# Turning normalised tokens of three groups by 32x32 blocks on VectorE and through device memory, in place of TensorE turns

**Chip, cores, metric.** One core of one Trainium2 chip. The metric is the device time of one execution, in microseconds (us). "Clock" is the clock that TensorE was granted, 1.0 being full. Profiles are of single executions, so a span differs from the median of the runs: by 5.0 in before.

## The reference

Attention with decay, in chunks of 64 positions, for 4 batches of 768 tokens; its output is the input of a mixing block: a Fourier transform along the tokens and along the 512 features, added to the input, then a normalisation, then a perceptron of two layers.

```python
def _moe_ref(x, w_ch1, w_ch2):
    X = np.fft.fft(np.fft.fft(x, axis=1), axis=2)
    u = x + np.real(X).astype(np.float32)
    mu = np.mean(u, axis=-1, keepdims=True)
    var = np.mean((u - mu) ** 2, axis=-1, keepdims=True)
    un = (u - mu) / np.sqrt(var + 1e-06)
    ch = np.maximum(un @ w_ch1, 0.0) @ w_ch2          # 512 -> 2048 -> 512
    return (u + ch).astype(np.float32)
```

The kernels take `un @ w_ch1` with the features of the normalised tokens `un` on the partitions (L636 of the kernel before, pm<-ut,w), so each 128x512 tile is turned first. This change is about who turns it.

## The kernel before

Tokens come in groups of two 128-token tiles. The first four groups are "plain" (ordinary products); in order of use they are called first, second, third and fourth plain group. All later groups ("late") already take the way through device memory. The perceptron runs in two halves of its hidden width; the second weight's first half is converted from the given 64-bit form in 512-column pieces, whose last three are called c5, c6 and c7. The "folds" are VectorE's additions (L426 to L484) that prepare a batch's tokens for the Fourier transform, in a first and a second part.

```python
ep = front_pool("ep", 2)          # two tiles "e" in all
up = plain_pool("up", 3)          # turned tokens "ut", three tiles
...
def load_weights(dst, src):       # one piece; VectorE's and ScalarE's passes
    raw = hp_.tile(...); e = ep.tile([128, 2 * WP], U16, tag="e")
    pw, sg = ...                  # both lie in e
    nc.sync.dma_start(raw, src.bitcast(U32))
    nc.scalar.activation(sg, top.bitcast(I16), AF.Sign)                      # L216
    nc.vector.tensor_scalar(pw, top, 0x7FF0, ...)                            # L217
    nc.scalar.activation(pw, pw, AF.Relu, bias=cvt[:, 0:1], scale=8.0)       # L218
    nc.vector.tensor_tensor(p, p, sg, op=ALU.mult)                           # L220
    nc.vector.tensor_scalar(d, hi, 0x000FFFFF, 0x00100000, ...)              # L222
    nc.vector.scalar_tensor_tensor(dst, lo, 2.0 ** -32, d, ...)              # L224
    nc.vector.scalar_tensor_tensor(dst, dst, 2.0 ** -20, p, ...)             # L225
...
def norm(g):
    ...
    plain = (b, g) in PLAIN
    if plain: ut = uts[b, g] = new(up, [128, KO, G * 128], "ut")
    else:     to = utd[b, g] = dram.tile([128, KO, G * 128], F32)
    for i in range(G):
        un = ...                                                             # L564, VectorE
        if plain:
            pt = psum_a([128, KO, 128])
            for c in range(KO):
                nc.tensor.transpose(pt[:, c, :], un[:, 128*c:128*c+128], ident)   # L569
            nc.scalar.copy(ut[:, :, 128 * i:128 * i + 128], pt)              # L573
        else:
            uq = new(ep, [128, DM], "e")                                     # the same pool of two
            nc.vector.transpose(uq, un)                                      # L577
            for r in range(0, 128, 32):
                nc.sync.dma_start(dst, src)                                  # L581, four stores a tile
...
run(beside(mix, 24.0, beside(att1, 2.75 * t_chunk, w, 0.16 * NW), 0.16 * NW + 1.75 * t_chunk))
half = [[mlp(b, g, h * FO // 2, (h + 1) * FO // 2) for b, g in PLAIN[:3]] for h in range(2)]
```

A scheduler places the instructions on each engine when the kernel is built, and an edit in one place moves others (in x12, with eight stores off its queue, k is issued 27 us sooner than in x3). SyncE issues 225 of the 276 transfers of before, in one queue, one after the other.

## Time and profile before

| | before |
|---|---|
| median of 3 runs | 824.45 us (822.53 to 825.08) |
| profiled run, span | 819.4 us, clock 1.0 |
| TensorE busy | 795.2 us, 97% |
| turns on TensorE (L569) | 32, of which 24 are for the second to fourth plain group |

The prediction below shows the main rows. First, one stretch from the first turn of the first plain group to the first product of a late group, which does the same work in all kernels but for the turns, and leaves out the start, whose length varies (the first turn is at 91.91 us in x9 and at 95.46 in after). Columns: start:end, length, then busy time of PE, PEld, DVE, ACT and POOL with instruction counts, then clock, DMA share, GB/s.

```profile
92.88:428.13 335.25, 328.28 (x1907) 229.87 (x1907) 214.93 (x464) 87.20 (x207) 49.03 (x57) 1.00 0.42 111
```

TensorE idles for 335.25 - 328.28 = 6.97 us in it.

SyncE's queue before a later attention chunk:

```profile
181.24 0.38 SPq L263 DMA_DIRECT2D k<-in_k_dram  x1
```

TensorE takes this k at 192.32 us, 11.1 us after its issue.

### The profile page before, as it was taken

The page shows a single profiled execution, that of the slowest core. Times are in us where ns is not written, and L with a number is a line of the kernel's source. Part 1 is how long each engine was busy: PE and PEld are TensorE (multiplying, and loading weights), DVE is VectorE, ACT ScalarE, POOL GpSimd, SP SyncE. Part 2 cuts the span into 40 slices and gives each one's busy share as a digit, 9 for nine tenths or more (in the row PEclk, how much of TensorE's full clock was granted, in tenths as well). Part 3 has the DMA queues.
Part 4 walks back from the last instruction along what each step waited for, and adds up shares of the span by engine and source line. Part 5 has one row for each costly group of instructions (what it writes and reads, how often), then busy time and mean ns, then how long its engine had stood idle before and what let it go on. Part 6 is the DMA issues. An engine that isn't in the chain of part 4 may idle for free.

```text
span 819.4 us, 11694 instructions
## 1 busy us (share of the span) xinstructions
PE 795.2 (97%) x4608; PEld 634.9 (77%) x4608; DVE 437.8 (53%) x1018; ACT 186.5 (23%) x448; POOL 86.1 (11%) x102
## 2 busy tenths in 40 slices
PE   6989899999999999999999999999999999999998
PEld 5777767768585857768648888888888888888886
DVE  5899798766743761354895541165313661146311
ACT  3756344225420211312002200022001210022100
POOL 3223340011011010220000000000000000000000
PEclk9999999999999999999999999999999999999999
DMA  9979624248741136530351011100111001010010
GB/s 233 249 154 271 174 90 129 63 113 201 203 125 51 52 62 131 129 123 26 93 162 42 1 53 51 52 1 1 64 40 52 0 1 39 33 33 0 1 39 26
DMA packets 126684, 68.88 MB, mean 84 GB/s; under 512 B 111150, under 2 KB 112174, under 8 KB 126630
## 3 DMA queue, kind: packets, MB, share of 16 engines
q1 hardware_dynamic: 121488, 55.67, 26.6%
q0 software_dynamic: 2112, 6.69, 2.4%
q10 hardware_dynamic: 3030, 5.78, 1.9%
q8 instruction: 36, 0.59, 0.3%
q14 instruction: 18, 0.15, 0.1%
HBM read 48.72 MB, written 19.40 MB: 83 GB/s over the span
## 4 chain that ended last, share of the span: by engine, by line
PE 80%; DVE 10%; issue 4%; DMA 3%; ACT 2%; POOL 1%; POOLq 0%; ACTq 0%; DVEq 0%
PE p L770 24%; PE p L723 24%; PE pm L650 10%; PE pm L636 8%; PE pa L332 3%; PE pa L516 3%; PE pa L298 3%; DMA x<-xb,ix 2%; PE pa L328 2%; PE pa L274 1%; DVE sc L302 1%; PE pa L315 1%; PE pa L348 1%; PE pa L279 1%; DVE stt L546 1%
## 5 line engine op out<-in xcount | busy, mean ns | idle before, releaser
L636 PE MATMUL pm<-ut,w 128*128 128x256 f32 x512 | 119.2, 382 | 0.0
L650 PE MATMUL pm<-w,hr 128*128 128x512 f32 x256 | 115.8, 597 | 0.2 <-DVE w L225 0.2
L636 PEld LDWEIGHTS pm<-ut,w 128*128 128x128 f32 x512 | 94.4, 190 | 15.4 <-issue 3.6
L723 PE MATMUL p<-ur,w 128*128 128x256 f32 x384 | 93.8, 379 | 0.0
L650 PEld LDWEIGHTS pm<-w,hr 128*128 128x128 f32 x256 | 46.6, 190 | 49.5 <-issue 48.0
L723 PEld LDWEIGHTS p<-ur,w 128*128 128x128 f32 x384 | 73.0, 190 | 10.3 <-issue 0.5
L723 PE MATMUL p<-us,w1s 128*128 128x256 f32 x256 | 65.7, 379 | 0.0
L770 PE MATMUL p<-w,hs 128*128 128x256 f32 x256 | 58.0, 379 | 0.5 <-DVE y L791 0.5
L770 PE MATMUL p<-w2s,hs 128*128 128x256 f32 x256 | 57.9, 379 | 0.0
L770 PE MATMUL p<-w,ha 128*128 128x256 f32 x256 | 57.9, 379 | 0.0
L770 PEld LDWEIGHTS p<-w,hs 128*128 128x128 f32 x256 | 48.5, 190 | 7.5 <-DVE y L791 0.9
L625 POOL DMA_INDIRECT out_dram<-y,ix x12 | 11.9, 989 | 402.6 <-DVE y L796 342.6
L770 PEld LDWEIGHTS p<-w2s,hs 128*128 128x128 f32 x256 | 48.6, 190 | 6.6
L723 PEld LDWEIGHTS p<-us,w1s 128*128 128x128 f32 x256 | 48.6, 190 | 6.6
L770 PEld LDWEIGHTS p<-w,ha 128*128 128x128 f32 x256 | 48.6, 190 | 6.6
L750 ACT COPY ha<-p 128x256 f32<-128x256 f32 x32 | 11.9, 372 | 169.1 <-PE p L723 139.4
L761 DVE TENSOR_TENSOR ha<-p,ha 128x256 f32<-128x256 f32 x32 | 13.6, 424 | 45.2 <-ACT ha L760 45.2
L298 PEld LDWEIGHTS pa<-qT,kT 64*128 64x128 f32 x384 | 26.0, 193 | 13.2 <-ACT qT L281 7.3
L302 DVE TENSOR_TENSOR sc<-pa,decay 128x512 f32<-128x512 f32 x48 | 31.5, 683 | 8.8 <-PE pa L298 8.5
L332 PE MATMUL pa<-sc,v 128*64 128x128 f32 x384 | 32.1, 284 | 4.1 <-DVE sc L302 4.1
L298 PE MATMUL pa<-qT,kT 64*128 64x128 f32 x384 | 30.7, 292 | 3.2 <-ACT qT L281 2.9
L270 POOL TENSOR_TENSOR kd<-k,decay 128x512 f32<-128x512 f32 x20 | 23.0, 1152 | 94.8 <-PE pa L315 64.5
(144 smaller groups left out, 1135.0 us busy)
## 6 DMA issues: line engine op xcount, KB each, us to landing
raw<-in_moe_w_ch_dram SPq DMA_DIRECT2D x32, 512.0 KB, 4.8
k<-in_k_dram SPq DMA_DIRECT2D x24, 256.0 KB, 5.0
q<-in_q_dram SPq DMA_DIRECT2D x24, 256.0 KB, 5.9
v<-in_v_dram SPq DMA_DIRECT2D x24, 256.0 KB, 4.9
ud<-x SPq DMA_DIRECT2D x16, 256.0 KB, 2.3
utd<-e SPq DMA_DIRECT2D x64, 64.0 KB, 2.2
u<-ud SPq DMA_DIRECT2D x16, 256.0 KB, 2.7
ur<-utd SPq DMA_DIRECT2D x6, 512.0 KB, 4.3
```

Of the source, the lines that this page charges most:

```text
L270: nc.gpsimd.tensor_tensor(kd, kt, kpow, op=ALU.mult)
L298: mm(pss[hi][:, hp, :], lhsT=kT[HD[hi], hp, :], rhs=qT[HD[hi], hp, :], start=True, stop=True)
L302: nc.vector.tensor_tensor(t, pss[hi], decay[:, hi::2, :], op=ALU.mult)
L328: mm(po[HD[hi], hp, :], lhsT=s_old[HD[hi], hp, :], rhs=qs[HD[hi], hp, :], start=(hp == 0), stop=False, skip_group_check=True)
L332: mm(po[HD[hi], hp, :], lhsT=vt[:, 2 * hp + hi, :], rhs=sc[hi][:, hp, :], start=(c == 0 and hp == 0), stop=(hp == HP - 1), skip_group_chec ...
L516: mm = nc.tensor.matmul(ps[0:m, n, :], lhsT=piece(a, i, n), rhs=cs[0:rows, a, i in (2, 3), n, :], start=(a == 0), stop=(a == 1))
L625: nc.gpsimd.indirect_dma_start(out=out.rearrange("b s d -> (b s) d"), out_offset=row_of(2 + HC * (b + 1) + T - HC), in_=y[:, :], in_offset ...
L636: nc.tensor.matmul(ps, lhsT=w1[:, c, 128 * fc:128 * fc + 128], rhs=ut[:, c, :], start=(c == 0), stop=(c == KO - 1))
L650: nc.tensor.matmul(ps, lhsT=hr[(fc - f0) // 4][:, fc % 4, 128 * i:128 * i + 128], rhs=w2[:, fc, :], start=(fc == f0), stop=(fc == f1 - 1))
L723: nc.tensor.matmul(ps, lhsT=s2.A[a][:, kt, 128 * i:128 * i + 128], rhs=U[b][:, kt, :], start=(first and kt == 0), stop=(kt == 1), skip_gro ...
L761: V.tensor_tensor(a22, two(Z), a22, op=ADD)
L770: nc.tensor.matmul(ps, lhsT=h[a][:, s, i, :], rhs=s2.B[b][:, i, :], start=(first and i == 0), stop=(i == HF - 1), skip_group_check=True)
```

## The change

Intent: take 24 turns, and six copies out of accumulators, off TensorE and ScalarE. The second to fourth plain groups go the way of the late ones: VectorE turns 32x32 blocks (0.70 us for a 128x512 tile, L577), four stores a tile put the blocks in place in device memory (0.63 us each to issue, L581), and one fetch per group brings the turned tokens back when the perceptron nears them.

```diff
-            plain = (b, g) in PLAIN
-            if plain:
+            plain, turned = (b, g) in PLAIN, (b, g) == PLAIN[0]
+            if turned:
                 ut = uts[b, g] = new(up, [128, KO, G * 128], "ut")
@@
-                if plain:
+                if turned:
                     pt = psum_a([128, KO, 128])
@@
+    def fetch(n):
+        if n < len(PLAIN):
+            ut = uts[PLAIN[n]] = new(up, [128, KO, G * 128], "ut")
+            nc.sync.dma_start(ut, utd[PLAIN[n]])
+
     def mlp(b, g, f0=0, f1=FO):
         ut = uts[b, g]
+        n = PLAIN.index((b, g))
+        if f0 == 0 and n < 2:
+            fetch(n + 1)
+        elif f1 == FO and n == 1:
+            fetch(3)
```

(Not shown: the pin on the first turn, which keeps its meaning.)

More of the change, by code (lines that the diff above doesn't have):

```diff
@@ L569, in norm @@
                         mm = nc.tensor.transpose(pt[:, c, :], un[:, 128 * c:128 * c + 128], ident)
-                        if (b, g, i, c) == (*PLAIN[0], 0, 0):
+                        if i + c == 0:
                             tc.keep_in_program_order(mm)
```

## The prediction

> **What bounds the kernel now.** I read the page first (busy shares), then busy time by stretches of 20 us, then the chain that ended last between 100 and 170 us, then each engine instruction by instruction from 92 to 205 us, where three of the four plain groups (two 128-token tiles each) are turned.
>
> ```profile
> PE 795.2 (97%) x4608; PEld 634.9 (77%) x4608; DVE 437.8 (53%) x1018; ACT 186.5 (23%) x448; POOL 86.1 (11%) x102
> ```
>
> TensorE is busy for all but 24 of 819.4 us: what it is spared counts where it has no gaps, and every new gap counts in full. By stretches (start:end, length; busy PE, PEld, DVE, ACT, POOL; clock, DMA share, GB/s):
>
> ```profile
> 100.00:120.00 20.00, 18.31 (x89) 13.38 (x88) 17.34 (x44) 9.33 (x23) 8.56 (x6) 1.00 0.26 85
> 120.00:140.00 20.00, 19.82 (x77) 12.56 (x76) 18.66 (x46) 7.63 (x16) 1.10 (x1) 1.00 0.40 124
> 140.00:160.00 20.00, 19.06 (x102) 15.20 (x101) 13.83 (x33) 6.07 (x19) 1.89 (x4) 1.00 0.24 79
> 160.00:180.00 20.00, 20.00 (x119) 11.84 (x117) 15.98 (x36) 5.59 (x11) 2.72 (x4) 1.00 0.37 74
> ```
>
> From 100 to 140 us VectorE is nearly as full as TensorE (36.0 of 40 us), although it has 53% over the span: the change puts work on VectorE exactly where it has least room. The chain there confirms it:
>
> ```profile
> 127.47 0.60 DVE w L224
> 128.07 0.34 DVE fo L483
> 128.41 0.34 DVE fo L484
> 128.74 0.61 DVE w L225
> 129.36 0.04 issue
> 129.40 1.12 PE pm L650 x2
> ```
>
> TensorE's second-layer product at 129.40 waits for the last step of converting one 512-column piece of the second weight (call the last three pieces of its first half c5, c6, c7); VectorE runs without a gap up to it. The removed work on TensorE:
>
> ```profile
> 147.63 0.76 PE L569 MATMUL pa<-ident,un 128*128 128x128 f32 x4 [0.94 <-DVE un L564]
> 148.23 1.03 PE L636 MATMUL pm<-ut,w 128*128 128x256 f32 x4
> 149.10 0.60 PE L569 MATMUL pa<-ident,un 128*128 128x128 f32 x4
> 149.54 0.39 PE L529 MATMUL pa<-dt,ys 128*128 128x128 f32 x2
> ```
>
> Starts at 149.10 and 149.54 show that four turns occupy TensorE for 0.44 us, 0.11 each: the 273 ns of a group's mean is latency. The bracket is a gap of 0.94 us in which TensorE waited for the tokens. An ordinary product has two records.
>
> Last, what the new path costs where it exists already, for the late groups (first a row of operations with min/median/max ns, then two rows of issues, KB each, us to landing, then a wait on ScalarE):
>
> ```profile
> L577 DVE STREAM_TRANSPOSE e<-un x16: 682/700/712, 159.0 to 419.7; 128x512 f32<-128x512 f32 x16
> ```
> ```profile
> utd<-e SPq DMA_DIRECT2D x64, 64.0 KB, 2.2
> ur<-utd SPq DMA_DIRECT2D x6, 512.0 KB, 4.3
> ```
> ```profile
> 164.74 0.67 ACT L216 ACTIVATE e<-raw 128x512 bf16<-128x512 int16 x1 [2.12 <-DMA utd<-e]
> ```
>
> The last row is the one to keep: tiles named e come from a pool of two, shared by turned tokens and weight conversion. A conversion here stood still for 2.12 us until four stores had emptied an e.
>
> [...]
>
> **The change part by part.**
>
> Removed: 24 of 32 turns on TensorE, 24 x 0.11 = 2.64 us; six ScalarE copies of 0.59 us, on an engine that is 23% busy: nothing. Gaps before those turns: 1.04 (at 101.74), 0.64 (113.76) and 0.94 us (147.63), 2.6 together. Also freed: two accumulator banks which the fourth group's turned tokens hold from 149 to 246 us (their copies come at 245.83, when the first group's buffer is free). TensorE has no gap from 160 to 240 us, so this is worth nothing. The upper bound of the gain is about 5.2 us.
>
> Added: six VectorE turns (6 x 0.62 us in steady flow = 3.7 us), 24 stores on the SyncE queue (some 0.63 us each to issue), three fetches of 512 KB (4.3 us each). The fetches are issued early: the second group's would land at about 121, wanted after 124; the fourth's some 60 us ahead. Hidden.
>
> Moved: the built order shows that the scheduler brought the width products (L529 to L534) forward, ahead of the first group's first layer, and pushed the conversion of c5, c6, c7 back behind the turns of both groups. I worked that order through with the durations above. Steps on VectorE: 0.60 us for a 512-column pass, 0.335 for a half, 0.62 to 0.65 for a turn, 1.16 from the statistics over GpSimd to the scaling.
>
> TensorE: width products end at 98.0, 32 first-layer products of 0.43 us at 111.8, c0 to c4 for two tiles (10 x 0.86) at 120.4, so 4 us ahead of before.
>
> VectorE: statistics of the second group ready 100.3, its turns end 103.4 and 105.6; statistics of the third group 107.8, its turns end 111.4 and 112.7. The third group's first e is emptied by four stores issued from 111.5, landing at about 115.7 to 116.3, and only then does c5 start (0.4 for one pass, ScalarE's 0.7 + 0.72 beside it, then two VectorE passes): ready 118.2 to 118.9. c6 takes the same e after c5 and is woven with folds: ready 123.3 to 124.0. c7 comes behind both blocks of the second fold (some 20 passes, about 8.5 us) and two passes of the next piece: ready 135.2 to 135.9, before 129.3.
>
> So TensorE waits about 1.5 us for c6, and, having done one more product group, from 127 until 135.5 for c7: about 8.5 us. Against before it is then 6.2 us later with 0.86 us more done: 5.3 us behind. To 161 us it saves eight turns (0.9) and the gap of 0.94: about 3.5 us behind.
>
> Then 160 to 200 us. The fourth group's two turns and eight stores (8 x 0.63 = 5 us of SyncE) stand in the same in-order queue ahead of the other two groups' stores, two weight loads and the next k, q, v. In before those loads were issued at 181.2 and used at 192.3 after 5.0 us of landing: 6 us to spare. By the same working k is issued at about 189.5, lands at 194.5, wanted at about 193.5 to 194.5: up to 1 us. ScalarE's conversion passes wait for stores in front of the copies that free accumulators: 1 to 2 us more. I add 1.5 for this part.
>
> Sum: +3.5 + 1.5 = +5 us, 824.5 becomes about 829. After 240 us TensorE's order is the same product for product in both builds, so nothing further changes; the last two thirds only shift.
>
> **The rivals.** (a) The plain gain: the waits stay hidden, TensorE loses 2.6 us and some gaps: 819.5 to 822. For it: fetches have time, VectorE is at 53% over the span. Against: VectorE's 36 of 40 us just there, and the e pool of two. (b) Only the c7 stall, with later loads arriving in time: about 826 to 828. (c) The queue is worse than I worked out: [...]every k, q, v is late and attention runs with gaps: 833 to 840. Against it: each later load has several us of slack, and the queue catches up between chunks. (d) The freed banks let attention run ahead; worth nothing while TensorE is full.
>
> **Range and chances.** My sum rests on the c7 stall (6 us, whose length is mostly counted VectorE passes) less sure savings, so most weight lies on (b) and the sum, 825 to 832. (a) sets the low end at 820.5, (c) the high end at 837. Two per cent is 16.5 us: a gain of that size is not there (upper bound 5.2 us), chance 0.01; a loss needs all of (c), chance 0.04; within 2%: 0.95. Predicted 828.5.
>
> **What would show it.** Right: TensorE records of L569 drop from 32 to 8; TensorE busy sum falls by about 2.6 us while its gaps grow by about 7; gaps between 120 and 137 us before second-layer products, put down to the conversion passes; waits for utd stores of some 2 to 3 us at 112 to 116 us on VectorE and ScalarE; the second group's second layer starting 3 to 4 us later than 157.4. Wrong: if c7 is ready before 131 us, the stall step fails and (a) holds; if the first gap is before the second group's first layer, the fetch was not hidden; if the lag is made at 180 to 200 us instead, the queue was the matter; if it is made up again between 240 and 300 us, where 2.7 us of gaps exist, the shift was not rigid.

## More of the kernel before

Second, TensorE at the product with c7 (start, duration, engine, line, operation, tiles, shapes, count; in brackets the idle time before and what ended it):

```profile
129.40 1.12 PE L650 MATMUL pm<-w,hr 128*128 128x512 f32 x2 [0.17 <-DVE w L225]
130.36 2.79 PE L516 MATMUL pa<-cs,fe 128*128 128x193 f32 x16
```

Piece c7 is ready 0.17 us late: the schedule is tight, with nothing to spare.

## The result, and the profile after

| | before, same chip | after |
|---|---|---|
| median | 822.23 us (820.44 to 825.08, 6 runs) | 834.37 us (832.46 to 836.05, 6 runs) |
| profiled span, clock | 819.4 us, 1.0 | 833.9 us, 0.989 |

The ratio is 1.0139 (95% interval 1.0115 to 1.0164): slower by 12 us, but inside 2%. Ratios here are the mean time of one kernel's runs over the mean of the other's of the same rounds, so not quite the ratio of the medians.

The same stretch of after, from the first turn to the first late product:

```profile
95.46:442.35 346.89, 328.24 (x1884) 229.60 (x1883) 219.11 (x470) 84.93 (x201) 44.41 (x57) 0.98 0.45 116
```

It is 346.89 - 335.25 = 11.6 us longer, and so holds nearly the whole loss. TensorE's idle time in it grew from 6.97 to 18.65 us, by 11.7. Its busy time did not fall, although 24 turns are gone: the clock column says why, 0.98 in place of 1.00. Part of the work ran slower.

Where the idle time lies, TensorE after (rows with a gap, and the row behind the longest):

```profile
127.28 1.98 PE L660 MATMUL pm<-w,hr 128*128 128x512 f32 x4 [2.26 <-DVE w L225]
139.30 2.08 PE L660 MATMUL pm<-w,hr 128*128 128x512 f32 x2 [8.31 <-DVE w L225]
141.17 3.99 PE L516 MATMUL pa<-cs,fe 128*128 128x193 f32 x16
...
204.00 0.63 PE L274 MATMUL pa<-ident,k 128*128 128x128 f32 x4 [2.65 <-DMA k<-in_k_dram]
```

There are waits of 2.26 us for c6 and of 8.31 us for c7, both ended by the last pass of a conversion, and one of 2.65 us for the next chunk's k. With one of 0.76 us for ScalarE (not shown) they make 14.0 us. Compare the two rows behind the c7 wait with those of before: the same products took 2.08 in place of 1.12 us, and 3.99 in place of 2.79. The windows show the reason (second last columns: clock, DMA share, GB/s):

```profile
120.00:132.00 12.00, 8.73 (x24) 4.10 (x22) 11.09 (x27) 4.34 (x8) 0.00 (x0) 1.00 0.73 226
132.00:140.00 8.00, 0.70 (x1) 0.50 (x2) 8.00 (x21) 1.81 (x4) 0.00 (x0) 0.59 0.06 12
140.00:146.00 6.00, 6.00 (x21) 4.68 (x20) 5.93 (x14) 3.33 (x7) 0.00 (x0) 0.70 0.48 162
```

While TensorE stood idle the granted clock fell to half, and stayed there until 143.6 us. In windows of 1 us it is 0.5 or 1.0, with a mixture only where it changes. It is at half again from 205.1 to 208.5 us, behind the wait for k. Each window's busy time times (1 - clock), summed over the stretch, is 3.9 us lost while working; before has 0.0. After was at half clock in these three stretches before its end,

```profile
27.56:30.98 3.42, 3.42 (x23) 3.09 (x20) 2.88 (x7) 1.75 (x4) 0.67 (x1) 0.50 0.87 195
133.38:143.62 10.24, 4.32 (x10) 3.29 (x11) 10.24 (x27) 3.27 (x6) 0.00 (x0) 0.50 0.18 56
205.06:208.47 3.41, 3.41 (x15) 2.49 (x15) 3.08 (x7) 2.10 (x6) 0.01 (x1) 0.50 0.67 213
```

which are 3.42, 10.24 and 3.41 us long, one, three and one times 3.41 us, and start 105.82 and 71.68 us apart, 31 and 21 such steps. TensorE worked in them for 3.42, 4.32 and 3.41 us.

VectorE after, the rows that make the waits:

```profile
114.66 0.71 DVE L577 STREAM_TRANSPOSE e<-un 128x512 f32<-128x512 f32 x1
119.76 0.43 DVE L217 TENSOR_SCALAR e<-raw 128x512 uint16<-128x512 uint16 x1 [4.40 <-DMA utd<-e]
...
121.52 0.69 DVE L225 SCALAR_TENSOR_TENSOR w<-w,e 128x512 f32<-128x512 f32 x1
...
126.55 0.68 DVE L225 SCALAR_TENSOR_TENSOR w<-w,e 128x512 f32<-128x512 f32 x1
...
138.56 0.68 DVE L225 SCALAR_TENSOR_TENSOR w<-w,e 128x512 f32<-128x512 f32 x1
```

Read it from the top. The last turn of the third group fills an e. The conversion of c5 (L217) then idles 4.40 us until stores have emptied an e. The three L225 rows are c5, c6 and c7; between c6 and c7 VectorE has not one gap, but works off the second fold (30 rows left out here, 24 of them from L426 and the passes after it), which the scheduler now puts ahead of c7. So the e pool makes the first wait and VectorE's order makes the second.

SyncE after:

```profile
181.69 0.40 SPq L209 DMA_DIRECT2D raw<-in_moe_w_ch_dram  x1
190.64 5.70 SPq L581 DMA_DIRECT2D utd<-e  x8
...
197.58 0.39 SPq L263 DMA_DIRECT2D k<-in_k_dram  x1
```

Eight stores stand ahead of two weights and k. They are those of the batch's last late group; the fourth plain group's begin the sixteen at 159.82 us (not shown), since the tile `un` has one buffer and so the turns keep the program's order. From 182.1 to 190.6 us SyncE issued nothing: it waited for VectorE (first view, from the list of SyncE's waits: us, times, longest), until the first turn of that last group was done (second view):

```profile
SPq L581 <- DVE e L220: 8.8, 1, 8.8
```

```profile
189.91 0.71 DVE L577 STREAM_TRANSPOSE e<-un 128x512 f32<-128x512 f32 x1
```

(The profile names the pass beside the turn; the turn ends at 190.62.) In before this group's turns ran at 171.70 and 173.22. With a group more to turn, VectorE's built order has them behind the work of the next attention chunk. The eight issues then took 5.70 us: 0.63 each (median of all 88), and a wait for the second turn between them. So k was issued at 197.58 and TensorE got it at 204.00.

### The profile page after: what moved, and what is told of

Same layout as the page of the kernel before. It is cut to its first block, busy times and chain, and to the rows that moved or that the text cites.

```text
span 833.9 us, 11694 instructions
## 1 busy us (share of the span) xinstructions
PE 796.9 (96%) x4584; PEld 636.1 (76%) x4584; DVE 443.3 (53%) x1024; ACT 183.9 (22%) x442; POOL 81.7 (10%) x102
## 5 line engine op out<-in xcount | busy, mean ns | idle before, releaser
L646 PEld LDWEIGHTS pm<-ut,w 128*128 128x128 f32 x512 | 94.9, 190 | 16.7 <-issue 3.3
L302 DVE TENSOR_TENSOR sc<-pa,decay 128x512 f32<-128x512 f32 x48 | 31.3, 685 | 11.7 <-PE pa L298 11.6
L332 PE MATMUL pa<-sc,v 128*64 128x128 f32 x384 | 32.9, 290 | 4.4 <-DVE sc L302 4.3
L298 PEld LDWEIGHTS pa<-qT,kT 64*128 64x128 f32 x384 | 25.1, 193 | 14.0 <-ACT qT L281 6.9
L332 PEld LDWEIGHTS pa<-sc,v 128*64 128x64 f32 x384 | 24.2, 142 | 12.2 <-DVE sc L302 6.1
L298 PE MATMUL pa<-qT,kT 64*128 64x128 f32 x384 | 29.8, 291 | 3.7 <-ACT qT L281 2.9
```

The costliest lines, as they stand in the source:

```text
L298: mm(pss[hi][:, hp, :], lhsT=kT[HD[hi], hp, :], rhs=qT[HD[hi], hp, :], start=True, stop=True)
L302: nc.vector.tensor_tensor(t, pss[hi], decay[:, hi::2, :], op=ALU.mult)
L332: mm(po[HD[hi], hp, :], lhsT=vt[:, 2 * hp + hi, :], rhs=sc[hi][:, hp, :], start=(c == 0 and hp == 0), stop=(hp == HP - 1), skip_group_chec ...
L646: nc.tensor.matmul(ps, lhsT=w1[:, c, 128 * fc:128 * fc + 128], rhs=ut[:, c, :], start=(c == 0), stop=(c == KO - 1))
```

## The experiments

Twelve kernels ran, and all give the reference's result. Theory A, stated first: the loss is made by added work in two orders that had little slack (none before c7, some 6 us before k). VectorE's order and the pool of two e delay c5 to c7; SyncE's order delays k. Its rivals are named where they are tested. Medians of before, on the chips concerned: 821.3 us for x1 to x4 (7 runs), 820.8 for x5 to x8 (7 runs), 822.7 for x9 to x12 (11 runs).

### x1: turned tokens in tiles of their own

The second and third group's turned tokens go to free tiles of the ut pool; only the fourth's stay in e.

```diff
+            own = (b, g) in PLAIN[1:3]
+            if own:
+                uqs = new(up, [128, KO, G * 128], "ut").rearrange("p c (i n) -> p (c i n)", i=G)
@@
-                    uq = new(ep, [128, DM], "e")
+                    uq = uqs[:, DM * i:DM * i + DM] if own else new(ep, [128, DM], "e")
```

> The changed kernel, but the turned tokens of the second and third plain group go into free buffers of the ut pool, not into the pool of two tiles e which the weight conversion uses too; the fourth group's still go into e. Theory A (the conversions of c5 to c7 stand behind the turned tokens' stores because they share e): VectorE's wait of 4.4 us before c5 is gone, TensorE's gap before c6 (2.26 us) too, the gap before c7 (8.31 us) falls to 3 to 5 us because c7 still stands behind the folds; median about 827. Theory B (the six turns' time on VectorE is enough by itself): the gaps before c6 and c7 stay within 1.5 us of 10.6 together, median 833 to 835.

Measured: 829.26 us (826.08 to 832.37, 4 runs), ratio 1.0083 (1.0057 to 1.0109). TensorE:

```profile
119.44 7.11 PE L663 MATMUL pm<-w,hr 128*128 128x512 f32 x16 [1.88 <-DVE w L225]
131.41 2.07 PE L663 MATMUL pm<-w,hr 128*128 128x512 f32 x2 [3.13 <-DVE w L225]
```

Without the shared tile VectorE's 4.40 us wait is gone and the c7 wait fell from 8.31 to 3.13 us, in the expected range; theory B falls. The c6 wait (first row) did not go, as was expected, but is 1.88 us: c6 came 5.6 us sooner, counted from the first turn, but the scheduler also put its first product after six products in place of twelve. The time came out 2 us above the expectation, and its runs spread over 6 us. They follow the clock roughly: 826.08 us at a mean clock of 0.996, 828.34 at 0.996, 830.18 at 0.994, 832.37 at 0.989. In the profiled run, the slowest, the half clock lasted from 130.5 to 140.7 us, so that sixteen products took 5.35 us and not 2.79. The shorter wait thus cost more in lost clock: behind its 3.13 us TensorE worked at half clock from 131.4 to 140.7 us, about 4.7 us lost by these times, against 2.2 us lost behind the 8.31 us of after.

### x2 and x3: only some of the groups

x2 moves the second and third group and leaves the fourth on TensorE; x3 does the opposite.

```diff
-   plain, turned = (b, g) in PLAIN, (b, g) == PLAIN[0]
+   plain, turned = (b, g) in PLAIN, (b, g) in (PLAIN[0], PLAIN[3])    # x2; in x3: in PLAIN[:3]
```

(and the fetches of the groups concerned)

> Only the second and third plain group are moved; the fourth is turned by TensorE as before. Theory A with its second part (the fourth group's stores hold the next k behind them in the SyncE queue): the gaps before c6 and c7 stay at 10 to 11 us, the gap of 2.65 us before the k transposes near 200 us is gone, and so are the slow products after it; median 829 to 831. If the k gap comes from the lag of the first part, it stays, and the median is 833 to 835.

> Only the fourth plain group is moved; the first three are turned by TensorE as before. Theory A: no gap before c6 and at most 1 us before c7, as before; k late near 190 to 200 us by 1 to 3 us; median 822 to 826. If the fourth group's move is harmless by itself, 820 to 822.

Measured: x2 833.83 us (830.49 to 837.21, 4 runs), ratio 1.0143 (1.0102 to 1.0184); x3 825.34 us (824.99 to 827.14, 4 runs), ratio 1.0055 (1.0038 to 1.0073). TensorE in x2, then in x3:

```profile
125.86 2.81 PE L658 MATMUL pm<-w,hr 128*128 128x512 f32 x4 [2.15 <-DVE w L225]
137.89 2.08 PE L658 MATMUL pm<-w,hr 128*128 128x512 f32 x2 [6.62 <-DVE w L225]
```

```profile
193.38 0.63 PE L274 MATMUL pa<-ident,k 128*128 128x128 f32 x4 [2.34 <-DMA k<-in_k_dram]
```

The two losses part cleanly: the waits for the conversion come with the second and third group, the wait for k with the fourth. In x2 the gaps were as expected and the time was 3 to 5 us above: half clock cost 8.1 us while working, as in x1 (8.1): 6.4 us in the stretches from 126.9 to 130.3 and 133.7 to 147.4 us, and 1.7 more from 307.8 us, after a gap of 1.58 us far from the change. No expectation so far had priced the half clock behind the c7 wait; x5 tests it.

### x4: the added work without the gain

The kernel before, still turning on TensorE, with VectorE's turns and the stores of the three groups added for nothing, and no fetch. Rival C holds that the fetches come late and hold TensorE up; here there are none.

```diff
                     nc.scalar.copy(ut[:, :, 128 * i:128 * i + 128], pt)
+                    if (b, g) != PLAIN[0]:
+                        uq = new(ep, [128, DM], "e")
+                        nc.vector.transpose(uq, un)
+                        for r in range(0, 128, 32): ... nc.sync.dma_start(dst, src)
```

> The kernel before, with the turn on VectorE and its stores added for the three groups for nothing: TensorE still turns them and nothing is fetched. Theory A says that what is added costs and what is removed saves little: gaps before c6 and c7 as in the changed kernel, median 834 to 839. Theory C (the fetched tokens come late, so TensorE waits for the round trip through device memory): no fetch, so the median stays at 822 to 826.

Measured: 837.96 us (836.18 to 839.74, 4 runs), ratio 1.0209 (1.0186 to 1.0231). The two long waits are there, 8.71 us before c7 and 2.79 us for k, put down to the same releasers as in after. The one before c6 is not: TensorE, which still has its turns to do, comes later.

So C falls. x4 is 16.7 us above its own before, after 12.1 above its own: 4.5 us apart, about what the saved turns can be worth (4.2, below). In the profiles x4 lost less to half clock, 1.6 us against 3.9.

### x5: work in the gap

Nine products for nothing, pinned between the c6 and the c7 products of the changed kernel. Theory H: the idle stretch is what halves the clock. Rival J: the clock dips for another reason.

```diff
             for fc in range(f0, f1):
+                if (b, g, i, fc) == (*PLAIN[0], 0, 7):
+                    pf = psum_a([128, DM])
+                    for k in range(9):
+                        mm = nc.tensor.matmul(pf, lhsT=hr[0][:, 0, 0:128], rhs=w2[:, 0, :], start=True, stop=True)
+                        tc.keep_in_program_order(mm)
```

> The changed kernel with nine products of 128x512 for nothing on TensorE (about 0.87 us each, 7.9 us together), pinned between the c6 products and the c7 product, where TensorE idled for 8.3 us; nothing else changed. Theory H (the idle stretch before c7 is what halves TensorE's granted clock for the next 4 us): the gap before c7 shrinks from 8.3 us to under 2, the granted clock stays 1.0 from 130 to 150 us, the sixteen fold products there take 2.8 us and not 4.0; the time falls by about 2 us, to 832 (830 to 835), although the work has grown. Rival J (the clock dips for other reasons[...] and would dip as much with the gap filled): the half-clock stretch near 140 us is still there, and the fillers run in it; the time is that of the changed kernel, 834, or more.

Measured: 832.03 us (831.38 to 833.48, 4 runs), ratio 1.0125 (1.0092 to 1.0159).

```profile
126.37 1.12 PE L665 MATMUL pm<-w,hr 128*128 128x512 f32 x2 [2.08 <-DVE w L225]
127.34 7.89 PE L663 MATMUL pa<-w,hr 128*128 128x512 f32 x18
...
138.39 1.12 PE L665 MATMUL pm<-w,hr 128*128 128x512 f32 x2 [0.58 <-DVE w L225]
139.35 2.79 PE L516 MATMUL pa<-cs,fe 128*128 128x193 f32 x16
```

```profile
132.00:140.00 8.00, 7.42 (x24) 4.18 (x23) 8.00 (x21) 1.84 (x5) 0.00 (x0) 1.00 0.36 108
140.00:146.00 6.00, 6.00 (x35) 5.10 (x34) 5.53 (x14) 3.69 (x8) 0.00 (x0) 1.00 0.36 118
```

With 7.9 us of useless work added, the c7 product is back at 1.12 us and the sixteen fold products at 2.79. H holds, J falls. In time, the interval overlaps that of after, so the gain of some 2 us is not settled by the runs. The clock is, and not in one profile alone: the mean clock is 0.996 to 0.998 in all four runs, and 0.989 to 0.994 in all six of after. This profile had a dip of its own, 70 to 74 us, before the change's place, after a gap of 1.29 us.

### x6 and x8: one more piece converted early

To get c7 ahead of the second fold, one more piece is converted in an earlier stage, in the changed kernel (x6) and, as a control, in the kernel before (x8). The turned tokens of x6 are still in e.

```diff
-    run(beside(mix, 24.0, beside(att1, 2.75 * t_chunk, w, 0.16 * NW), 0.16 * NW + 1.75 * t_chunk))
+    run(beside(mix, 24.0, beside(att1, 2.75 * t_chunk, w, 0.2 * NW), 0.2 * NW + 1.75 * t_chunk))
```

> The changed kernel with one more weight piece converted in the stretch before the folds (share 0.20 of the weights in place of 0.16), so that in VectorE's order c7 stands before the second fold and not behind it; the turned tokens still share e. Theory A (VectorE's order and the two tiles of e make the stall): the c7 gap falls from 8.3 to under 3 us, since c7's conversion no longer waits behind the second fold, though c5 or c6 still wait for the stores by up to 4 us in e; 826 to 831. Rival (the stall is the device-memory path itself, and moves with it): the gap stays at 6 to 9 us and the time at 833 to 836.

> The kernel before with the same earlier conversion and nothing else: the control for x6 and x7. Its small waits before c5 to c7 are already under 1 us, so both theories expect no more than 1 us of change, 820 to 823. If it falls by 2 us or more, what x7 gains over the kernel before is the conversion's place and not the moved turns.

Measured: x6 833.25 us (827.88 to 833.44, 4 runs), ratio 1.0118 (1.0071 to 1.0164); x8 826.50 us (825.75 to 827.76, 4 runs), ratio 1.0054 (1.0022 to 1.0085). Both times missed. In x6 the c7 wait is gone (0.53 us is left), so VectorE's order was indeed what made it. But k, which waited 2.65 us in after, now waits 6.51:

```profile
200.87 1.09 PE L274 MATMUL pa<-ident,k 128*128 128x128 f32 x4 [6.51 <-DMA k<-in_k_dram]
```

Counted from the first turn, TensorE came to k's place 6.3 us sooner than in after and k only 2.5 us sooner: most of a wait removed in one place stood up again in the next. And the early piece has a price of its own, which x8 shows alone. Its control expectation, "no more than 1 us", was wrong: TensorE waits for the first normalised tokens,

```profile
94.25 0.67 PE L569 MATMUL pa<-ident,un 128*128 128x128 f32 x4 [2.94 <-DVE un L564]
...
97.39 1.97 PE L328 MATMUL pa<-qs,st 64*64 64x128 f32 x14
```

and then works at half clock from 95 to 102 us (3.3 us lost). VectorE's order at this place is the same in before, conversion passes included. What differs is TensorE's: in before it fills this time with the attention's products,

```profile
90.00 1.09 PE L328 MATMUL pa<-qs,st 64*64 64x128 f32 x16 [0.75 <-DVE qs L285]
```

which in x8 the scheduler put behind the turns.

### x7: the same, without the shared tiles and without the fourth group

x1's own tiles, x2's choice of groups, x6's early piece.

> Only the second and third plain groups moved, their turned tokens in free buffers of their own pool, and one more weight piece converted before the folds: every cost that theory A names is taken away (no wait for stores in e, c7 before the second fold, no late k). The 16 turns (1.8 us) and some of their gaps leave TensorE. Theory A: no gap of over 1.5 us on TensorE from 105 to 210 us, granted clock 1.0, 818 to 821, the first version below the kernel before (821 to 822). If the gain of the removed turns is worth nothing on this path: 821 to 824.

Measured: 825.62 us (824.51 to 825.71, 4 runs), ratio 1.0046 (1.0015 to 1.0077). From 105 to 210 us its largest gap is 1.00 us, as expected; the miss of 5 us is x8's price, a gap of 2.57 us and half clock from 92 to 99. Against its control x8 it is 0.9 us shorter, which the runs do not tell from none.

### x9 and x10: the extra piece in a better place

The extra piece comes after the first plain group's tokens: x9 is otherwise x7, x10 is the kernel before. Rival K: VectorE's added turning comes back as a wait whatever the order.

```diff
+    run(part(w, 1.0))
     half = [[mlp(b, g, h * FO // 2, (h + 1) * FO // 2) for b, g in PLAIN[:3]] for h in range(2)]
```

> As x7 (only the second and third plain groups moved, their turned tokens in free buffers of their own pool), but with the extra weight piece converted after the first plain group's normalised tokens and not ahead of them, where in x7 and x8 it made TensorE wait 2.6 to 2.9 us at 92 to 94 us and then run some 6 us at half clock (3 us lost). In VectorE's order c7 still stands before the second fold. Theory A: no gap over 1.5 us from 85 to 210 us, no half clock there, and the 16 turns' 1.8 us with some of their gaps gained: 818 to 821 against 821 before. Rival K (VectorE's added 2.8 us of turning reappear as a wait of 1.5 to 3 us at c5 to c7, whatever the order): 821 to 825.

> The kernel before with the same later place of the extra piece: the control of x9. Its c5 to c7 waits were under 1 us, so nothing is to be gained: 820 to 823. Its wait for the first normalised tokens should be at most 1 us (2.9 in x8).

Measured: x9 820.49 us (818.78 to 822.89, 6 runs), ratio 0.9980 (0.9957 to 1.0002); x10 821.59 us (820.57 to 822.87, 6 runs), ratio 0.9987 (0.9965 to 1.0009). The largest gap of x9 between 85 and 210 us is 1.12 us, before a product with a piece of the second weight, and there is no half clock. K falls. The second and third group then gain about 1 us over the control, which the runs do not tell from none.

### x12 and x11: k's queue

x12 is x3 with the fourth group's eight stores issued by GpSimd. x11 is the changed kernel with all three groups moved and everything mended: own tiles, the extra piece as in x9, and these eight stores on GpSimd.

```diff
-                        nc.sync.dma_start(dst, src)
+                        (nc.gpsimd if (b, g) == PLAIN[3] else nc.sync).dma_start(dst, src)
```

> As x3 (only the fourth plain group moved; 825.3 us, with a wait of 2.34 us for k and 3.8 us at half clock after it), with that group's stores issued by GpSimd in place of SyncE. If k is late because eight issues of 0.71 us stand ahead of it on SyncE's queue: no wait for k over 1 us, no half clock, 820 to 822. If its landing is late: unchanged, 824 to 827.

> All three groups moved as in the changed kernel, with every named cost mended: own buffers for the second and third group, the extra piece as in x9, and the fourth group's eight stores issued by GpSimd, so that the next k stands behind none of them on SyncE's queue. Theory A with the k step: the waits at c5 to c7 and for k are each under 1 us, no half clock from 85 to 210 us, 24 turns (2.6 us) and their gaps (up to 2.6 us) gained: 816 to 820. Rival: k stays late (the landing, not the issue, is what is late[...]): a gap of 2 to 3 us with half clock after it, 821 to 826.

Measured: x12 818.59 us (817.86 to 821.74, 6 runs), ratio 0.9953 (0.9929 to 0.9977); x11 818.67 us (818.24 to 819.43, 5 runs), ratio 0.9950 (0.9927 to 0.9974). Both are below the kernel before, by half a per cent, and x12 below its expected range. Three of the 11 runs of before are at a mean clock of 0.996 and took over 825 us; the other eight have a median of 822.4 us, and the control x10 has 821.6, so the gain without half clock is 3 to 4 us. SyncE in x3, then in x12 (x3's eight stores are again the last late group's; the sixteen of x12 are those of both late groups):

```profile
180.34 5.70 SPq L581 DMA_DIRECT2D utd<-e  x8
...
187.29 0.38 SPq L263 DMA_DIRECT2D k<-in_k_dram  x1
```

```profile
160.47 0.38 SPq L263 DMA_DIRECT2D k<-in_k_dram  x1
...
165.64 15.21 SPq L581 DMA_DIRECT2D utd<-e  x16
```

The wait for k is gone. But the step is not the clean one expected: k is issued 27 us sooner, not 5.7, since with eight stores off its queue the scheduler also put k ahead of the late groups' sixteen stores. TensorE takes this k sooner too, at 185.13 us (192.32 in before). That k stood behind those stores is shown as the cause of its wait; that the fourth group's eight issues are any part of it is not. Issue time alone was not the matter in after: SyncE waited 8.8 us for the data of the stores ahead of k, and the eight issues took 5.70 us. The stores took no less time to land (3.2 us from GpSimd, 2.2 from SyncE).

The same stretch as above, first turn to first late product, in the profiles of x9, x10, x11 and x12:

```profile
91.91:425.87 333.96, 326.32 (x1892) 228.47 (x1892) 216.15 (x469) 83.83 (x202) 44.28 (x57) 1.00 0.45 116
```

```profile
92.07:427.53 335.46, 328.36 (x1907) 229.84 (x1907) 214.32 (x465) 86.66 (x206) 49.75 (x57) 1.00 0.42 109
```

```profile
93.30:425.52 332.22, 324.55 (x1883) 226.56 (x1883) 217.07 (x471) 82.74 (x200) 50.84 (x65) 1.00 0.47 120
```

```profile
94.05:425.93 331.88, 325.59 (x1899) 228.39 (x1899) 216.33 (x466) 85.56 (x205) 55.09 (x65) 1.00 0.44 115
```

Against before's 335.25 us: -1.3, +0.2, -3.0, -3.4. In x11, TensorE's busy time fell by 3.7 us for 24 turns, and idle time grew by 0.7. x12 gains as much with only 8 turns moved; summed by operation its busy time shows 1.4 us less of turns, and about 1.3 us less in the attention's products (L298 and L332), as x11's does. Why those are shorter is open. x11's 16 further turns take 2.5 us more off TensorE, but it idles 1.4 us longer than x12 and its other products count 1.5 us more; why is open. No run gives the kernel before an earlier k alone, so how much of the gain of x11 and x12 is the moved turns' is not shown.

## Why the prediction was right and wrong

The time, 834.4, lies in the stated range of 820.5 to 837 and within 2%, as forecast. That is in part luck: it is above 825 to 832, where most of the weight lay, and in the band of rival (c), every k, q and v late, which did not happen. The mechanism was right in the main: waits for the conversion, put down to VectorE, and no trouble with the fetches. The loss was too small: +5 predicted (from 824.5, 2 us above the 822.2 of the later runs), +12 measured (+11.6 in the stretch, which is used here). Each step, counted from the first turn so that the start's noise drops out:

- **TensorE ahead at c0 by 4 us.** Right. The first second-layer product came 23.3 us after the first turn in before and 19.1 in after.
- **The e pool, c5 and c6: 1.5 us of wait.** Right in kind, 2.26 in size. VectorE stood still for 4.40 us, where the working allowed about 3, so c5 and c6 came near 1 us later than worked out.
- **c7 behind the second fold: 8.5 us of wait, 5.3 us behind.** The wait was 8.31. Counting VectorE's passes in the built order gave it. TensorE was 43.84 - 36.52 = 7.3 us later, with 0.9 more done: 6.5 behind.
- **From there to 161 us only savings, 3.5 us behind.** This step failed. The gap of 0.94 and eight turns were saved as said, but the c7 wait halved TensorE's clock until 143.6 us, 2.2 us lost, and at the third marker (the second group's second layer) after was 70.90 - 64.48 = 6.4 us behind. The prediction priced a gap at its length; x5 shows that a gap also slowed what followed (the c7 product took 2.08 us behind the gap and 1.12 with the gap filled).
- **k up to 1 us late, 1 to 2 us on ScalarE's copies: 1.5.** This term was mis-sized most. The wait for k was 2.65 us. The stores' issue time was right, 0.63 us. But the last late group's stores began 15.6 us later than in before, behind a turn that VectorE's order had put late, so k was issued 13.8 us later (102.12 against 88.36) where the working had 8.3; TensorE was ready for it only 6.5 us later (105.89 against 99.44); and k needed 6.4 us from issue to use where 5.0 was allowed. Nothing in the prediction has SyncE waiting for that turn. ScalarE's share was 0.76. With 1.7 us of half clock behind it the place cost 5.1 us, 3.6 more than the term. This is what rival (c) had named, the queue, although not with k, q and v late in every chunk: one chunk was.
- **Removed: 24 x 0.11 = 2.64 us.** Too low by the trace's count. TensorE's busy time for turns fell by 4.2 us (5.7 for 32 in before, 1.5 for 8 in after), about 0.17 each. This counts each group of four to its end, which may overlap what follows (in the prediction's rows 0.60 us from 149.10, with the next start at 149.54). All of TensorE's busy time in the stretch, less the half clock's 3.9 us, fell by about as much, 3.9.
- **A rigid shift after 240 us.** Right: after is behind by 14.1 us at 269 us, 14.2 at 428 and 14.5 at the end, of which 2.6 are the start's.
- **Rival (d), the freed accumulator banks, worth nothing.** No run contradicts it, none isolates it.
- **The stores' 2.2 us to landing.** Right for the stores that SyncE issues: 2.2 us in after as well (median). The eight that GpSimd issued in x12 took 3.2 us.

The sum that closes: idle time +11.7, half clock +3.9, turns -4.2, together +11.4 against 11.6 measured. (Idle and busy time make up the stretch by definition; what this tests is the split of the busy time.) By place, what the predicted +5 lacked: 1.2 up to c7, 1.9 of waits at k, 3.9 for the clock; less 0.5 that was saved beyond the working between c7 and 161 us.

## What to carry to other kernels

When you move work from the full engine to one with room on average, build the change and read the order on the receiving engine and on the transfer queue at that very place: here 0.17 us of waiting became 8.3, and a k stood 8.8 us behind stores that waited for their data. Price a new TensorE gap of over 2 us at more than its length, since the work after it may run at half clock: here it did behind 11 of the 14 such gaps listed in the last section, and in three profiles behind a gap of 1.29 to 1.59 us. When a change loses for such reasons, mend them before you drop it. With tiles of its own, one conversion moved, and stores off the loads' queue, the same three groups ran in 818.7 us, below the kernel before. Then take the mended orders without the change too: x12 reached the same with 8 turns moved in place of 24, so the gain is not shown to be the turns'.

## Gaps, half clock and the time of an issue, as measured here

- Gaps of over 2 us on TensorE, from 60 us on, in after and x1 to x8, where the clock behind them was read: all 5 of over 3.1 us were followed by half clock (3.13 us in x1, 6.51 in x6, 6.62 in x2, 8.31 in after, 8.71 in x4), and so were 6 of the 9 between 2 and 3 us (2.15 in x2, 2.34 in x3, 2.57 in x7, 2.65 in after, 2.76 in x1 and 2.94 in x8 were; 2.08 in x5, 2.26 in after and 2.79 in x4 were not). Three shorter ones were followed by half clock as well, 1.29 us in x5, 1.58 in x2 and 1.59 in x1, but 1.57 in x9, x11 and x12, 1.58 in after and 1.59 in before were not. So under 3 us the length of the gap alone did not tell in these runs whether half clock would follow. In after, cut from 20 us to its last stage into the steps of 3.41 us that its half-clock stretches mark, the three steps at full clock in which TensorE idled most, 53.7% of the step from 24.15 us, 69.9% from 129.96 and 69.0% from 201.64, were followed by half clock, and no other was; the next, 44.8% from 123.14 with the gap of 2.26 us, was not. What decides it beyond this one trace is not shown. Nor was the time at half clock the same: it lasted 4 us of work behind the c7 wait in after, but 9 us of unbroken work in x1 (131.4 to 140.7) and in x2 (137.9 to 147.4).
- SyncE took 0.63 us to issue one store of 64 KB with 128-byte runs (median, in before and in after).
